# Where small VectorE operations stand in an attention loop: the first batch's routing and the early conversions moved to the steps that carry products of P and v

## The chip, the cores and the metric

The kernel runs on 1 core of one Trainium2 chip. The metric is the device time of one execution in microseconds. TensorE (PE) does the matrix products and transposes, VectorE (DVE) and ScalarE (ACT) the elementwise work, GpSimd (POOL) elementwise work and some DMAs, SyncE (SP) issues most DMAs. Each engine works through its own list of instructions in order and waits for others by semaphores.

## The reference

Three parts run one after the other (fp32 results):

```python
# attention over 2 batches, 8 heads, 768 tokens, 64 wide, masked by cluster
q_assign = argmax(normalised q . centroids); k_assign = the same for k
scores = where(q_assign == k_assign, q @ k.T / 8, -1e9)
x = softmax(scores) @ v              # -> 1536 tokens x 512
# mixture of 8 experts, each token to the one with the largest logit
e_idx = argmax(x @ w_gate)
x = gate * sigmoid(x @ w_output_gate)[e_idx] * (relu(x @ w1[e]) @ w2[e])
# dense block
h = x @ w_in;  out = (h * sigmoid(1.702 h)) @ w_out     # 512 -> 2048 -> 512
```

`w_in` and `w_out` arrive as float64.

## The kernel before

**The attention loop.** The work of two heads of a batch is a unit, eight units in all (0 to 3 batch 0, 4 to 7 batch 1). A unit has 12 steps, so the loop variable `i` runs over 96 steps and two more; a step is 128 queries of one head. Here a step's place in its unit is r, so that i = 12u + r. The order of instructions on every engine is written by hand (`manual_schedule`). In one pass of the loop at `i` these are issued: the scores of step i+1 on PE (L515, L516) and their row maximum on DVE (`nm`, L518); small pieces of preparation for the next unit; in some passes a few conversion operations (`convert_early`); one entry of `av`, a third of a unit's products of P and v (PE, L567), if one is queued; the transposes of step i-1 (PE, L532), each half copied out of PSUM by ACT (L537) and by DVE (L539), in `emit_pt`; and the exponential of step i+1 on ACT (L524). The scores have two PSUM buffers, so scores of a step wait for the exponential of two steps before. The transposes have two PSUM buffers of half a step each.

**Steps with products.** From unit 1 on, `av` holds something in the passes r = 2, 3, 8 and 9 (every third step and the one after it), 24 PE instructions each. In r = 3 and 9 the product's result is then copied by ACT (`oa`, L573). At r = 2 the cluster scores of the next unit follow (PE, `pcl`, L418), which DVE transposes (L421) and works on (L391 to L400). At r = 9 ACT makes the rows `ohT` (L429) and SP sends eight small DMAs (L435) into `Q` and `Z` of the next unit. At r = 10, 11, 0 and 1 the next unit's q and k are transposed on PE (`pqk`, L337), in the PSUM buffer of the products, which is free when `oa` has been copied.

**Routing of the first batch.** `route(0)` is a generator that chooses an expert for each of the first 768 tokens, ranks them and computes places. It is appended to `routing` at i = 61 and advanced by `advance(2)` after each of the two copies in `emit_pt`, so four parts a step. A part is mostly one DVE operation of a few columns. Three empty parts (`WAITS`) stand ahead of its small matmuls `prk`. Some of its operations (`sbase`, `srev8`, `span`, `soon`) give the address at which a block of fp32 rows is read later; SP reads `soon` in registers at i = 78. At the end six blocks of rows `xs` are scaled on POOL (L741) and scattered by POOL's indirect DMAs (L746), four parts each.

**Conversions.** The first two of the eight pieces of w_in and w_out are converted from float64 bits to fp32 during the attention. They are eight loads of 128x1024 words (`raw`), two of them held at a time. Each has four operations: `bits` (ACT squares the high words into `csq`, L125; DVE shifts, L126), `top` (L129), `tail` (L132), and `last`, which is DVE's `guard` on `csq` (L135), POOL's DMA of `csq` to DRAM (L176, `wd`) and the next load on SP (L113). `slots` says how many operations a pass issues. The target of the square is one buffer until i = 48, then two in turn:

```python
            hold, ops = wide_ops(cva, t, spare_squares[(4 * c + g) % len(spare_squares)])
...
        if i == NS // 2:
            assert len(fill) == E
            spare_squares.append(zrow)
```

After the attention come the second batch's routing, the experts and the dense block; nothing in them is edited.

Of the kernel before, what the change touches and what calls it, by code (L numbers as in the profile page):

```python
# [14 lines left out]
ALU = mybir.AluOpType  # L15
AX = mybir.AxisListType
# [7 lines left out]
E = 8  # L24
DFF = 2048
T = S // 128
# [20 lines left out]
def attention_moe_ffn(ctx: ExitStack, tc: tile.TileContext, q, k, v, centroids, w_gate, w_og, w1, w2, w_in, w_out, out):  # L47
    nc = tc.nc
# [11 lines left out]
    rev8 = const.tile([128, E], F32, name="rev8")  # L60
    ebase = const.tile([128, E], F32, name="ebase")
    iota8 = const.tile([128, E], F32, name="iota8")
# [16 lines left out]
    soon = const.tile([1, 2], I32, name="soon")  # L79
    gone = const.tile([128, E], F32, name="gone")  # L80
    ngone = const.tile([128, 1], F32, name="ngone")
    sbase = const.tile([128, E], F32, name="sbase")
    srev8 = const.tile([128, E], F32, name="srev8")
    span = const.tile([128, 3], F32, name="span")
    soonh = const.tile([128, E], F32, name="soonh")
# [79 lines left out]
    def convert_early():  # L165
        if not convert:
            if not ready:
                return
            c, g, t = ready.popleft()
            if not spare_squares:  # L170
                spare_squares.append(cva.tile([128, 512], F32, name="csq", tag="csq", bufs=1))
            hold, ops = wide_ops(cva, t, spare_squares[(4 * c + g) % len(spare_squares)])

            def last(f=ops[3]):
                f()
                nc.gpsimd.dma_start(out=wd[2 * c + g // 2][:, (g % 2) * 512:(g % 2) * 512 + 512], in_=hold["s"])  # L176
                load_early()
            convert.extend(ops[:3] + [last])
        convert.popleft()()
# [311 lines left out]

    TAIL, WAITS = 3, (3, 2, 0)
    BITS = (3, 10, 3)
    steps = [(u, h, j) for u in range(len(UNITS)) for h in range(2) for j in range(T)]

# [1 line left out]
    NS = len(steps)  # L499
# [26 lines left out]
    def emit_pt(i):  # L526
        L = live[i]
        j = steps[i][2]
        for n in range(2):
            pt = ps_t.tile([128, 512], F32, name="pt", tag="pt")  # L530
            for r in range(3):
                nc.tensor.transpose(pt[:, r * 128:(r + 1) * 128], L["P"][:, n, r * 128:(r + 1) * 128], ident)  # L532
            src = pt[:, :384].rearrange("p (r c) -> p r c", r=3)
            qs = slice(128 * (j % 3), 128 * (j % 3) + 128)
            dst = L["pT"][:, 3 * n:3 * n + 3, qs]
            if n == 0:
                nc.scalar.copy(dst, src)  # L537
            else:
                nc.vector.tensor_copy(dst, src)  # L539
            advance(2)  # L540

    KTS = (range(0, 3), range(3, T))
    av = deque()
# [52 lines left out]


    rt = {}


    GROUPS = ((0, 0, T), (1, 0, T // 2), (1, T // 2, T // 2))
# [4 lines left out]
    def route(gi):  # L606
# [62 lines left out]
        if gi == 0:  # L669
            nc.vector.tensor_tensor(dest, rk, ebase[:, None, :].to_broadcast([128, nj, E]), op=ALU.add)  # L670
            lm, lv, c0 = new("lm", [128, 1]), new("lv", [128, E]), new("c0", [128, E])
            nc.vector.tensor_copy(c0, part)
            yield
            nc.vector.scalar_tensor_tensor(lk, c0, float(E), rev8, op0=ALU.mult, op1=ALU.add)
            yield
            nc.vector.tensor_reduce(lm, lk, op=ALU.max, axis=AX.X)
            yield
            nc.vector.tensor_scalar(soonh, lk, lm, None, op0=ALU.is_equal)
            yield
            nc.vector.tensor_tensor(lv, soonh, c0, op=ALU.mult)  # L680
            yield
            nc.vector.tensor_reduce(ngone, lv, op=ALU.add, axis=AX.X)
            yield
            nc.vector.tensor_scalar(ngone, ngone, float(FIRST), None, op0=ALU.min)
            yield
            nc.vector.tensor_scalar(gone, soonh, ngone, None, op0=ALU.mult)
            yield
            nc.vector.scalar_tensor_tensor(sbase, gone, -1.0, ebase, op0=ALU.mult, op1=ALU.add)
            yield
            nc.vector.scalar_tensor_tensor(srev8, gone, -float(E), rev8, op0=ALU.mult, op1=ALU.add)  # L690
            yield
            nc.vector.tensor_tensor(lv, soonh, ebase, op=ALU.mult)
            yield
            nc.vector.tensor_reduce(span[:, 1:2], lv, op=ALU.add, axis=AX.X)
            yield
            nc.vector.tensor_tensor(span[:, 0:1], span[:, 1:2], ngone, op=ALU.subtract)
            yield
            nc.vector.tensor_copy(soon[:, 1:2], span[0:1, 0:1])
            nc.vector.tensor_tensor(lv, soonh, iota8, op=ALU.mult)
            yield  # L700
            nc.vector.tensor_reduce(lm, lv, op=ALU.add, axis=AX.X)
            yield
            nc.vector.tensor_copy(soon[:, 0:1], lm[0:1])
            yield
            nc.vector.tensor_tensor(dest, dest, gone[:, None, :].to_broadcast([128, nj, E]), op=ALU.subtract)
        else:
            nc.vector.tensor_tensor(dest, rk, sbase[:, None, :].to_broadcast([128, nj, E]), op=ALU.add)
# [16 lines left out]
        if gi == len(GROUPS) - 2:  # L724
            lm, lv = new("lm", [128, 1]), new("lv", [128, E])
# [6 lines left out]
        for j in range(nj):  # L732

            if b == 0:
                xs = pp.tile([128, DM], F32, name="xs", tag="xs", bufs=2)
            else:
                xs = xw[0][:, j0 + j].rearrange("p h c -> p (h c)")[:, :DM]
            dst = xs.rearrange("p (h d) -> p h d", h=H)
            src, g = xw[b][:, j0 + j, :, 0:D], gate[:, j:j + 1]
            if gi == 0:  # L740
                nc.gpsimd.tensor_scalar(dst, src, g, None, op0=ALU.mult)  # L741
            elif gi == 1 or j % 2:
                nc.scalar.activation(dst, src, AF.Copy, scale=g)
            else:
                nc.vector.tensor_scalar(dst, src, g, None, op0=ALU.mult)
            x = nc.gpsimd.indirect_dma_start(  # L746
                out=xd[:, :], out_offset=bass.IndirectOffsetOnAxis(ap=di[:, j:j + 1], axis=0),
                in_=xs, in_offset=None).ins
            nc.gpsimd.engine_nop()
            tc.declare_no_dep(x, group="rows", reason="every token has a row of its own")  # L750
            tc.add_to_no_dep_group("rows", x)
            for _ in range(3 if gi == 0 else 0):
                yield
            for y in fill:
                tc.add_manual_dep(x, y.name, DATA_DEP, reason="rows are zero first")
            scatters.append(x.name)
            yield

    sooner = {}

# [84 lines left out]
    def advance(n=1000, stop=0):  # L845
        while n > 0 and routing:
            n -= 1
            x = next(routing[0], 0)
            if x == 0:
                routing.pop(0)  # L850
            elif x == stop:
                break
# [77 lines left out]
            for f in pieces[u][n]:  # L930
                f()

    slots = {12 * u + r: n for u in range(2, 6) for r, n in ((3, 1), (8, 1), (9, 2))}
    slots.update({21: 3, 27: 1, 75: 1, 80: 1, 81: 2, 86: 3, 87: 2, 92: 2, 93: 2})

    weights = soon_weights()
    soon_at = {78: [soon_ids], 84: [soon_rows, lambda: next(weights)], 87: [lambda: next(weights)], 91: [soon_x]}
# [17 lines left out]
    for i in range(NS + 2):  # L955
        nu, r = divmod(i + 3, 12)
        if i == 3 or r == 0 and nu + 2 < len(UNITS):
            load_unit(nu + 2)
        prepare(i, True)
        if i + 1 < NS:  # L960
            emit_scores(i + 1)
        tail = i >= NS - TAIL
        if (tail or i % 3 == 0) and ost:
            ost.popleft()()
        prepare(i)
        if i == 0:
            spots[:] = [(ps_m, "m")]
        if i >= 14 and i % 4 == 2 and len(fill) < E:
            zero_rows(len(fill))
        if i % (NS // 2) == NS // 2 - 4 and i < NS:  # L970
            sum_logits(i // (NS // 2))
        if i == NS // 2 + 13:
            routing.append(route(0))
        for f in soon_at.get(i, ()):
            f()
# [3 lines that stand above are left out]
        if i in (15, 18):  # L979
            load_early()  # L980
        for _ in range(slots.get(i, 0)):
            convert_early()
        for _ in range(2 if tail else 1):
            if av:
                av.popleft()()
        prepare(i, False, True)
        if 0 <= i - 1 < NS:
            emit_pt(i - 1)
        n = i - (1 if tail else 2)
        if 0 <= n < NS and steps[n][2] % 3 == 2:  # L990
            queue_av(n)
        if i + 1 < NS:
            emit_exp(i + 1)
# [358 lines left out]
    with tc.manual_schedule():  # L1352
# [14 lines left out]
        for g in range(G + 2):  # L1367
            e, c = divmod(g, 8)
            nxt = wins.get(e + 1)
            r = c - (7 - nxt["nr"]) if nxt else 0  # L1370
# [94 lines left out]
    with tc.manual_schedule():  # L1465
        gq = deque()
        for g in range(len(seq) + 2):
# [6 lines left out]
            if g >= 2:  # L1474

                for m in range(4) if g < len(seq) or g == len(seq) + 1 else ():
                    cuts = (slice(0, DM // 2), slice(DM // 2, DM)) if g == len(seq) + 1 and m == 3 else (slice(0, DM),)
                    for cs in cuts:
                        for g0, gh, gl in list(gq)[:1] if g < len(seq) else gq:
                            fh, tb, c, i = seq[g0]  # L1480
# [47 lines left out]
```

## Time and profile before

| what | value |
|---|---|
| time, median of 3 runs | 724.02 us (720.78 to 724.78) |
| time of the profiled execution | 724.04 us |
| span of its trace | 722.3 us |
| PE / PEld / DVE / ACT / POOL busy | 97% / 80% / 63% / 54% / 37% of the span |
| units 4, 5 and 6 of the attention | 29.50, 31.53 and 31.02 us |

The span runs from the first to the last instruction; the profiled execution's own time is 1.74 us longer. Busy shares are means over parts with different limits: PE is busy nearly all of the attention, DVE more in the attention than later. Times of a unit run from the start of its first row maximum to the next unit's first.

### The profile page before, as it was taken

The page shows a single profiled execution, that of the slowest core. Times are in us where ns is not written, and L with a number is a line of the kernel's source. Part 1 is how long each engine was busy: PE and PEld are TensorE (multiplying, and loading weights), DVE is VectorE, ACT ScalarE, POOL GpSimd, SP SyncE. Part 2 cuts the span into 40 slices and gives each one's busy share as a digit, 9 for nine tenths or more (in the row PEclk, how much of TensorE's full clock was granted, in tenths as well). Part 3 has the DMA queues.
Part 4 walks back from the last instruction along what each step waited for, and adds up shares of the span by engine and source line. Part 5 has one row for each costly group of instructions (what it writes and reads, how often), then busy time and mean ns, then how long its engine had stood idle before and what let it go on. Part 6 is the DMA issues. An engine that isn't in the chain of part 4 may idle for free.

```text
span 722.3 us, 12542 instructions
## 1 busy us (share of the span) xinstructions
PE 699.4 (97%) x4522; PEld 577.7 (80%) x4522; DVE 452.2 (63%) x888; ACT 393.0 (54%) x789; POOL 266.4 (37%) x219
## 2 busy tenths in 40 slices
PE   8999999999999998999999998999999999999996
PEld 6777776776766777999999898888888888888885
DVE  6969788899988972344544545788564666242322
ACT  7767676666766643566777676544434353222220
POOL 2230321303280033766979889222532112020202
PEclk8999999999999998999999999999999999999999
DMA  6768869546066538566677775233634220010101
GB/s 198 170 189 273 215 225 282 153 146 181 27 171 213 196 126 269 172 229 206 199 241 232 263 235 188 89 110 68 85 59 59 60 87 30 1 59 1 59 0 59
DMA packets 70573, 105.18 MB, mean 146 GB/s; under 512 B 9627, under 2 KB 48283, under 8 KB 70507
## 3 DMA queue, kind: packets, MB, share of 16 engines
q1 hardware_dynamic: 67563, 95.94, 45.7%
q0 software_dynamic: 2944, 8.40, 3.1%
q8 instruction: 37, 0.61, 0.3%
q14 instruction: 29, 0.24, 0.1%
HBM read 70.46 MB, written 14.69 MB: 118 GB/s over the span
## 4 chain that ended last, share of the span: by engine, by line
PE 54%; issue 17%; POOL 7%; DMA 7%; DVE 6%; ACT 6%; SPq 1%; POOLq 0%; ACTq 0%; DVEq 0%
PE po L567 6%; PE pt L532 5%; PE ph L1347 4%; PE ph L1349 4%; PE ph L1348 4%; PE py L1447 3%; PE py L1445 3%; PE py L1446 3%; PE sp L515 3%; PE sp L516 3%; POOL w L1067 3%; PE py L1162 3%; PE ph L1162 2%; ACT w L1064 2%; DMA raw<-in_moe_w_dram 2%
## 5 line engine op out<-in xcount | busy, mean ns | idle before, releaser
L1067 POOL TENSOR_TENSOR w<-raw,w 128x1024 fp32r<-128x1024 f32 x51 | 128.1, 2529 | 38.3 <-ACT w L1064 25.4
L518 DVE TENSOR_REDUCE nm<-sp 128x1 f32<-128x768 f32 x96 | 91.6, 955 | 15.6 <-PE sp L516 14.4
L1430 DVE TENSOR_TENSOR sg<-ph,sg 128x512 f32<-128x512 f32 x48 | 33.2, 691 | 99.7 <-ACT sg L1429 97.5
L524 ACT ACTIVATE P<-sp,nm 128x768 f32<-128x768 f32 x96 | 87.2, 909 | 10.6 <-DVE nm L518 10.1
L532 PEld LDWEIGHTS pt<-ident,P 128*128 128x128 f32 x576 | 65.2, 141 | 27.3 <-issue 16.9
L532 PE MATMUL pt<-ident,P 128*128 128x128 f32 x576 | 82.9, 277 | 3.4 <-DVE pT L539 1.6
L1429 ACT ACTIVATE sg<-ph 128x512 f32<-128x512 f32 x48 | 28.7, 597 | 104.8 <-PE ph L1349 100.4
L1447 PE MATMUL py<-w,gl 128*128 128x512 f32 (+1 forms) x194 | 75.2, 387 | 0.0
L1445 PE MATMUL py<-w,gh 128*128 128x512 f32 (+1 forms) x194 | 75.0, 387 | 0.0
L1446 PE MATMUL py<-w,gh 128*128 128x512 f32 (+1 forms) x194 | 75.0, 387 | 0.0
L1100 POOL TENSOR_TENSOR w<-csq,w 128x512 fp32r<-128x512 f32 x24 | 32.7, 1363 | 114.5 <-ACT w L1099 114.5
L1347 PE MATMUL ph<-yth,w 128*128 128x512 f32 x192 | 74.8, 390 | 0.0
L1349 PE MATMUL ph<-yth,w 128*128 128x512 f32 x192 | 74.7, 389 | 0.0
L1348 PE MATMUL ph<-ytl,w 128*128 128x512 f32 x192 | 74.7, 389 | 0.0
L515 PE MATMUL sp<-X,Q 128*128 128x384 f32 x192 | 73.6, 384 | 0.5 <-ACT P L524 0.4
L1162 PE MATMUL py<-ht,w 128*128 128x512 f32 (+6 forms) x224 | 69.8, 367 | 3.5 <-DVE room L1169 2.0
L1064 ACT CAST w<-raw 128x1024 fp32r<-128x1024 f32 x68 | 70.5, 1042 | 4.8 <-issue 2.5
L1162 PE MATMUL ph<-t,w 128*128 128x512 f32 (+6 forms) x224 | 68.9, 366 | 1.2 <-DVE ht L1186 0.7
L567 PE MATMUL po<-pT,ld_v 128*32 128x384 f32 x768 | 68.6, 490 | 0.0
L516 PE MATMUL sp<-Z,Q 80*128 80x384 f32 x192 | 65.3, 340 | 1.9 <-DMA Q<-ohT 1.9
L537 ACT COPY pT<-pt 128x384 f32<-128x384 f32 x96 | 45.9, 478 | 32.7 <-PE pt L532 32.7
L539 DVE COPY pT<-pt 128x384 f32<-128x384 f32 x96 | 52.8, 550 | 8.1 <-PE pt L532 7.7
(294 smaller groups left out, 1468.7 us busy)
## 6 DMA issues: line engine op xcount, KB each, us to landing
raw<-in_moe_w_dram SPq DMA_DIRECT2D x64, 512.0 KB
raw<-in_moe_w_in_dram SPq DMA_DIRECT2D x16, 512.0 KB
raw<-in_moe_w_out_dram SPq DMA_DIRECT2D x16, 512.0 KB
xd<-zrow SPq DMA_DIRECT2D x8, 768.0 KB
Q<-Hq SPq DMA_DIRECT2D x28, 192.0 KB
ew<-in_moe_w_dram SPq DMA_DIRECT2D x9, 384.0 KB
ld_q<-in_q_dram SPq DMA_DIRECT2D x8, 384.0 KB
ld_k<-in_k_dram SPq DMA_DIRECT2D x8, 384.0 KB
```

The lines of the kernel that those rows point to most:

```text
L515: nc.tensor.matmul(sp[:, n, :384], d["Q1"][:, h, cs], d["X"][:, h, ks], start=True, stop=False)
L518: nc.vector.tensor_reduce(nm, sp[:, :, :384], op=ALU.max, axis=AX.XY, negate=True)
L532: nc.tensor.transpose(pt[:, r * 128:(r + 1) * 128], L["P"][:, n, r * 128:(r + 1) * 128], ident)
L567: nc.tensor.matmul(po[32 * g:32 * g + 32, :384], v_[:, hh, tile_t(kt), 32 * a:32 * a + 32], pts[n][:, kt, :], start=kt < (2 if alone else ...
L1067: (eng or nc.gpsimd).tensor_tensor(lo, r, f32(hi), op=ALU.subtract)
L1162: nc.tensor.matmul(ps[:, :2 * n], w_hi, t, start=first, stop=False)
L1347: nc.tensor.matmul(ph, wa(key, 0, k, i), yth[:, k, cs], start=(k == 0), stop=False)
L1348: nc.tensor.matmul(ph, wa(key, 0, k, i), ytl[:, k, cs], start=False, stop=False)
L1349: nc.tensor.matmul(ph, wa(key, 1, k, i), yth[:, k, cs], start=False, stop=(k == 3))
L1445: nc.tensor.matmul(po[m][:, cs], gh[:, ms], wb(key, 0, i)[:, cs], start=first, stop=False)
L1446: nc.tensor.matmul(po[m][:, cs], gh[:, ms], wb(key, 1, i)[:, cs], start=False, stop=False)
L1447: nc.tensor.matmul(po[m][:, cs], gl[:, ms], wb(key, 0, i)[:, cs], start=False, stop=last)
```

## The change

The routing of batch 0 starts at i = 56, no longer at 61, and is no longer advanced in `emit_pt` (only the passes of the last six steps still are). A table `PACE` says how many parts a pass issues, ahead of the products: 4 at i = 56, 5 at 57, 8 at 62, 5 at 68 and one at each of 69 to 76. The three empty parts and those between scatters are gone. The nine operations for the fp32 rows' address become `soon_place`, issued at i = 74. Conversions move: `slots` gains passes at r = 2 and loses those at r = 8 from unit 4 on. The 32 operations stand in these passes, as pass:count. Before: 21:3, 27:1, 32:1, 33:2, 39:1, 44:1, 45:2, 51:1, 56:1, 57:2, 63:1, 68:1, 69:2, 75:1, 80:1, 81:2, 86:3, 87:2, 92:2, 93:2. After: 21:3, 26:2, 27:1, 32:1, 33:2, 38:2, 39:1, 44:1, 45:2, 50:2, 51:1, 63:1, 69:2, 81:2, 86:3, 87:2, 92:2, 93:2.

```diff
-    TAIL, WAITS = 3, (3, 2, 0)
+    TAIL, WAITS = 3, (0, 2, 0)
...
             else:
                 nc.vector.tensor_copy(dst, src)
-            advance(2)
+            if i >= NS - T:
+                advance(2)
...
     rt = {}
+    later = []
...
             nc.vector.tensor_scalar(gone, soonh, ngone, None, op0=ALU.mult)
             yield
-            nc.vector.scalar_tensor_tensor(sbase, gone, -1.0, ebase, op0=ALU.mult, op1=ALU.add)
-            yield
...
-            nc.vector.tensor_reduce(lm, lv, op=ALU.add, axis=AX.X)
-            yield
-            nc.vector.tensor_copy(soon[:, 0:1], lm[0:1])
-            yield
+            later.append((lm, lv))
             nc.vector.tensor_tensor(dest, dest, gone[:, None, :].to_broadcast([128, nj, E]), op=ALU.subtract)
...
-            for _ in range(3 if gi == 0 else 0):
-                yield
             for y in fill:
                 tc.add_manual_dep(x, y.name, DATA_DEP, reason="rows are zero first")
             scatters.append(x.name)
             yield
+
+    def soon_place():
+
+        lm, lv = later.pop()
+        nc.vector.tensor_tensor(lv, soonh, ebase, op=ALU.mult)
+        nc.vector.tensor_reduce(span[:, 1:2], lv, op=ALU.add, axis=AX.X)
+        nc.vector.tensor_tensor(span[:, 0:1], span[:, 1:2], ngone, op=ALU.subtract)
+        nc.vector.tensor_copy(soon[:, 1:2], span[0:1, 0:1])
+        nc.vector.tensor_tensor(lv, soonh, iota8, op=ALU.mult)
+        nc.vector.tensor_reduce(lm, lv, op=ALU.add, axis=AX.X)
+        nc.vector.tensor_copy(soon[:, 0:1], lm[0:1])
+        nc.vector.scalar_tensor_tensor(sbase, gone, -1.0, ebase, op0=ALU.mult, op1=ALU.add)
+        nc.vector.scalar_tensor_tensor(srev8, gone, -float(E), rev8, op0=ALU.mult, op1=ALU.add)
...
-    slots = {12 * u + r: n for u in range(2, 6) for r, n in ((3, 1), (8, 1), (9, 2))}
-    slots.update({21: 3, 27: 1, 75: 1, 80: 1, 81: 2, 86: 3, 87: 2, 92: 2, 93: 2})
+    slots = {12 * u + r: n for u in range(2, 6) for r, n in ((2, 2 if u < 5 else 0), (3, 1), (8, u < 4), (9, 0 if u == 4 else 2))}
+    slots.update({21: 3, 27: 1, 81: 2, 86: 3, 87: 2, 92: 2, 93: 2})
+
+    PACE = {8: 4, 9: 5, 14: 8, 20: 5, **{n: 1 for n in range(21, 29)}}
...
-        if i == NS // 2 + 13:
+        if i == NS // 2 + 8:
             routing.append(route(0))
...
             convert_early()
+        advance(PACE.get(i - NS // 2, 0))
+        if i == NS // 2 + 26:
+            soon_place()
         for _ in range(2 if tail else 1):
             if av:
                 av.popleft()()
```

## Rows read from the trace of the kernel before

**Rows 1.** Busy time by engine in units 4, 5 and 6 (us, count), then clock, DMA share, GB/s.

```profile
133.64:163.14 29.50, 29.32 (x250) 21.71 (x249) 24.85 (x41) 20.02 (x45) 6.56 (x10) 1.00 0.55 154
163.14:194.67 31.53, 29.85 (x258) 21.95 (x256) 29.90 (x80) 20.28 (x47) 7.43 (x9) 1.00 0.41 108
194.67:225.69 31.02, 29.31 (x248) 21.45 (x246) 25.21 (x41) 20.14 (x45) 21.08 (x20) 1.00 0.59 161
```

**Rows 2.** Waits of PE in unit 5: total us, times, longest.

```profile
PE pt L532 <- DVE pT L539: 0.9, 2, 0.5
PE prk L661 <- DVE cntb L639: 0.5, 1, 0.5
```

**Rows 3.** DVE's instructions by line in unit 5: busy us, mean ns, idle before.

```profile
L618 DVE TENSOR_TENSOR lgp<-lgp,xw 128x96 f32<-128x96 f32 x2 | 1.6, 814 | 0.0
...
L135 DVE SCALAR_TENSOR_TENSOR zrow<-zrow,ct 128x512 f32<-128x512 f32 x1 | 0.7, 682 | 0.0
...
L126 DVE TENSOR_SCALAR ct<-raw 128x512 int32<-128x512 int32 x1 | 0.4, 386 | 0.0
...
L634 DVE TENSOR_REDUCE cnt<-roh 128x8 f32<-128x48 bf16 x1 | 0.2, 239 | 0.0
```

**Rows 4.** Wait of PE in unit 6, the longest one.

```profile
PE sp L516 <- DMA Q<-ohT: 1.2, 1, 1.2
```

**Rows 5.** Timeline of SP near the end of unit 6: start us, us.

```profile
214.95 1.76 SPq L113 DMA_DIRECT2D raw<-in_moe_w_out_dram  x1
```

**Rows 6.** Timeline around pass i = 26: start us, us, idle before and releaser.

```profile
80.16 1.01 POOL L344 TENSOR_TENSOR Lk<-Fk,Hk 128x384 fp32r<-128x384 f32 x1
...
80.44 0.96 DVE L518 TENSOR_REDUCE nm<-sp 128x1 f32<-128x768 f32 x1 [0.22 <-PE sp L516]
...
83.12 0.58 DVE L421 STREAM_TRANSPOSE sc<-pcl 128x384 f32<-128x384 f32 x1 [1.72 <-PE pcl L418]
83.57 0.48 ACT L537 COPY pT<-pt 128x384 f32<-128x384 f32 x1 [2.79 <-PE pt L532]
...
83.94 0.91 ACT L524 ACTIVATE P<-sp,nm 128x768 f32<-128x768 f32 x1
...
87.20 0.42 PE L515 MATMUL sp<-X,Q 128*128 128x384 f32 x1
```

**Rows 7.** Timelines of POOL and ACT: three instructions on `csq` and `zrow`.

```profile
117.72 0.58 POOL L176 DMA_DIRECT2D wd<-csq  x1 [7.01 <-DVE rs L577]
...
125.58 0.69 ACT L125 ACTIVATE csq<-raw 128x512 f32<-128x512 f32 x1 [0.24 <-DMA wd<-csq]
...
177.62 0.56 POOL L176 DMA_DIRECT2D wd<-zrow  x1 [7.86 <-DVE rs L576]
```

**Rows 8.** POOL's DMA queue from 178.8 to 179.8 us: packets, MB, share.

```profile
q0 software_dynamic: 72, 0.23, 60.8%
```

**Rows 9.** The chain of waits in unit 5, one piece: start us, us.

```profile
171.56 3.66 DMA X<-Hk
```

**Rows 10.** Two stretches, columns as in rows 1.

```profile
82.00:84.00 2.00, 2.00 (x24) 1.18 (x17) 0.84 (x2) 0.43 (x2) 0.00 (x0) 1.00 0.90 242
102.00:104.00 2.00, 2.00 (x17) 1.93 (x16) 1.65 (x3) 1.95 (x5) 0.64 (x2) 1.00 0.15 37
```

**Rows 11.** Timeline around pass i = 33: start us, us, idle before and releaser.

```profile
99.68 0.68 DVE L129 SCALAR_TENSOR_TENSOR ct<-raw,ct 128x512 int32<-128x512 int32 x1
...
100.83 0.48 ACT L573 COPY oa<-po 128x384 f32<-128x384 f32 x1 [1.17 <-PE po L567]
...
101.66 0.91 ACT L524 ACTIVATE P<-sp,nm 128x768 f32<-128x768 f32 x1
...
102.12 0.49 PE L337 MATMUL pqk<-ident,ld_q 128*128 128x128 f32 x3
...
103.03 0.42 PE L515 MATMUL sp<-X,Q 128*128 128x384 f32 x1
```

**Rows 12.** Timeline of DVE after pass i = 56.

```profile
157.08 0.56 DVE L539 COPY pT<-pt 128x384 f32<-128x384 f32 x1 [0.47 <-PE pt L532]
```

More of the change, by code (lines that the diff above doesn't have):

```diff
@@ L687, in route @@
             yield
-            nc.vector.scalar_tensor_tensor(sbase, gone, -1.0, ebase, op0=ALU.mult, op1=ALU.add)
-            yield
-            nc.vector.scalar_tensor_tensor(srev8, gone, -float(E), rev8, op0=ALU.mult, op1=ALU.add)
-            yield
-            nc.vector.tensor_tensor(lv, soonh, ebase, op=ALU.mult)
-            yield
-            nc.vector.tensor_reduce(span[:, 1:2], lv, op=ALU.add, axis=AX.X)
-            yield
[L696 to L700, printed above, removed]
-            nc.vector.tensor_reduce(lm, lv, op=ALU.add, axis=AX.X)
-            yield
-            nc.vector.tensor_copy(soon[:, 0:1], lm[0:1])
-            yield
+            later.append((lm, lv))
             nc.vector.tensor_tensor(dest, dest, gone[:, None, :].to_broadcast([128, nj, E]), op=ALU.subtract)
@@ L751, in route @@
             tc.add_to_no_dep_group("rows", x)
-            for _ in range(3 if gi == 0 else 0):
-                yield
             for y in fill:
```

## The prediction

> **What bounds the kernel now.** I read the page first: PE is busy nearly everywhere, so an edit in the attention counts only where PE stands still or is stretched. Then I compared units by stretch, because the 12 steps of a unit repeat and an undisturbed unit is a ready measure of what the others lose. In [rows 1] unit 4 takes 29.50 us with 29.32 us of PE, unit 5 31.53 with 29.85, unit 6 31.02 with 29.31. The reader should see that units 5 and 6 are 2.03 and 1.52 us longer at the same full clock, and that DVE is busy for 29.90 of unit 5's 31.53 us. Third came PE's waits: in unit 5 they name DVE, the copy `pT` (0.9 us) and the cast `cntb` (0.5 us) [rows 2]; in unit 6 one wait of 1.2 us for the small DMAs into `Q` [rows 4]. Last came the timelines of the passes that receive the moved work.
>
> **What the change takes away.** Unit 5 holds the routing of batch 0: two additions of 0.81 us and some 36 small operations of at most 0.24 us [rows 3], which I count at 0.15 to 0.2 us each, between the copies that PE waits for. After the change no routing stands between copies there. What PE still does for it, 7 small matmuls, is about the 0.5 us by which unit 5's PE time exceeds unit 4's [rows 1]. So unit 5 gains 2.03 - 0.5 = 1.5 us (at most 2.0, at least 0.9 if only the waits on `pT` go).
>
> Unit 6 loses the `guard` at i = 75 and `bits` at 80, and the early load that is issued at 214.95 behind unit 7's stacked rows [rows 5]. That load of 0.5 MB runs just ahead of the small DMAs that PE then waits for. After the change it is issued at i = 69, before those rows. I take the whole wait, 1.2 us [rows 4]; bounds 0 (other transfers, POOL's scatters too, are late as well) and the 1.5 us by which the unit is long.
>
> **What the moved DVE work costs.** At r = 2 DVE waits 1.72 us for `pcl` [rows 6]. That idle time covers `guard` and `bits` at i = 26 and 50 (0.68 + 0.39 = 1.07 us [rows 3]), `top` and `tail` at 38 (two like the 0.68 us of [rows 11]), ten routing parts at 62 (ten by some 0.18 = 1.8 us) and the nine of `soon_place` at 74 (nine by 0.15 = 1.4 us). I cost them at nothing; without the cover they would be delays of 1.1 to 1.8 us each on the next row maximum. At i = 56 the two additions and two small operations make 1.63 + 0.4 = 2.0 us, against 0.39 us of `bits` removed and 0.47 us that the copy waits for PE [rows 12]: DVE falls 1.2 us behind. At 57 seven parts of 0.2 us replace `top` and `tail`, no change; at 68 eight of 0.18 us give 0.6 us of lag; at 69 1.07 us replaces 1.4. The lag meets a maximum whose exponential is not needed at once, so I take 0.3 us in all, between 0 and 1.8.
>
> At no cost: the scatters stay one a step in 69 to 74, since four parts a step with three empty ones became one. POOL does the same 12 instructions; its `wd` at 69 comes ahead of the first scatter, where it stood behind the last. `soon` is ready at 74, four passes before SP reads it; SP's queue behind it (the row DMAs) is not needed until unit 7. The removed empty parts are no instructions.
>
> **What the moved conversions add: ACT waits for a DMA.** Until i = 48 there is one target for the square, and piece 4 takes it again. At i = 26, 33 and 50 the pass issues `last` of one piece and `bits` of the next, both on `csq`. ACT's square must not overwrite `csq` before POOL's DMA has read it. That this wait is real is in [rows 7]: the DMA issued at 117.72 held the square back until 125.58, 7.9 us later, and it was five passes before. In the changed passes the two are in one pass, so ACT stands for the whole of DVE's `guard`, POOL's issue and the transfer. Behind it on ACT stand the copy `pT` and the exponential, and at i = 33 also `oa`; PE waits for all three.
>
> Let L be the time from the issue of `wd` to ACT's release. The lower bound is 2.1 us: issued at 177.62 in a quiet stretch [rows 7], its packets were through by 179.8 [rows 8]. The upper is 7.9 us.
>
> At i = 26 the maximum ends at 81.40, `guard` at 82.0, POOL is free (its L344 ends at 81.17), so `wd` starts at 82.1 [rows 6]. The square takes about 0.65 us, the copy 0.37 until the exponential starts, the exponential 0.91: it ends at 82.1 + L + 1.93 = 84.0 + L. The scores that need its buffer ran at 87.20 [rows 6]. PE loses L - 3.2 us. The DMA engines are 0.90 busy there [rows 10], with transfers of 192 KB; one of these took 3.66 us after its issue [rows 9]. `wd` has 256 KB, a third more, so I take L = 4.5: 1.3 us lost. Pass 50 has the same pattern in unit 4: another 1.3 us. The bounds are 0 and 4.7 us each.
>
> At i = 33 `guard` would stand where `top` starts, 99.68, end at 100.36, and `wd` start at 100.45 [rows 11]. The DMA engines are only 0.15 busy [rows 10], so L is near its lower bound, 2.2 us. The square runs from 102.65 to 103.3, `oa` to 103.7, `pT` to 104.1, the exponential to 105.0. The transposes `pqk`, which reuse the products' buffer, ran at 102.12 and would wait for `oa` until 103.7; the scores at 103.03 would wait until 105.0 [rows 11]. The larger counts: 2.0 us. With L = 4 it is 3.8 us. ACT has `oa` and, in the following passes, copies of `pqk` to do as well and does not catch up before PE has lost the time.
>
> The Trainium skill, in "DMA: Bandwidth & Descriptors", section "Anatomy of one DMA — SWDGE (gpsimd) path", gives a GpSimd DMA about 2.0 us plus its bytes over 436e3 per us; for 256 KB an estimate of 2.6 us. The quiet transfer agrees with it roughly, the one of 7.9 us does not. By that page the passes 26 and 50 would cost nothing and the sum below would be about 2 us lower, which is the first rival.
>
> **The sum.** Lost: 1.3 + 1.3 + 2.0 + 0.3 = 4.9 us. Gained: 1.5 + 1.2 = 2.7 us. Net 2.2 us longer. Against the profiled execution, 722.3 us of span and 1.74 us around it, 724.04 in all: 726.2 us. The median of the three runs is 724.02, so the same forecast holds for it. The attention ends before the experts' loads and products start, so I carry its difference to the end one to one. Differences under 0.5%, 3.6 us, can hardly be told from none.
>
> **Rivals.**
> *The transfers are short.* If L is at most 3.2 us at passes 26 and 50, only pass 33 costs: 2.0 + 0.3 - 2.7 = -0.4, or 723.6 us. For it speaks the quiet transfer [rows 7, 8], against it the DMA share of 0.90 [rows 10]. Chance 0.17. This is the case of the page's estimate.
> *The transfers are long.* If `wd` queues behind the stacked rows and loads as the one at 117.72 did, L is 7 at 26 and 50 (3.8 us each) and 4 at 33 (3.8): 11.4 + 0.3 - 2.7 = 9.0, or 733.0 us, slower. It decides from a total of waits of 6.0 us on, which with pass 33 as computed is L above 5.2. For it: two of the three passes lie where the DMA engines are nearly full; against it: 3.66 us for a smaller transfer in such a stretch [rows 9]. Chance 0.15.
> *PE has enough other work.* If the products that stand in these very passes cover all three waits and no DVE lag appears, the change does what it looks like: 2.7 to 3.5 us gained, 720.9 us. The 2.79 us that ACT waits for PE at r = 2 [rows 6] speak for it; at r = 9 there is only 1.17 us [rows 11], against it. Chance 0.13.
> *The forecast*, 726.2 us, has 0.55. Its own range is 723.5 to 729.5 (L from 3.5 to 6, the wait in `Q` gone or not).
>
> **Numbers.** The range 721.2 to 731 leaves out half of the last rival and most of the long transfers' upper part, about 0.2. Faster by over 0.5% (under 720.4) needs that last rival with unit 6 gaining more than its wait: 0.1 with what I may have overlooked. Slower by over 0.5% (over 727.6): the long transfers, 0.15, and the upper third of the forecast, 0.18: 0.33. The rest, 0.57, is no change that can be told.
>
> **What would show it.** Right: waits of ACT's L125 on the DMA of `wd` at three places, each 2 us or more, and behind them PE waits on ACT's `P`, `pT` or `oa` near passes 26, 33 and 50; units 2, 3 and 4 longer than 29.5 us by 1 to 2.5 us, unit 5 near 30.0, unit 6 near 29.8, no wait of L516 on `Q` in it. Wrong: no wait on L125, or one without a PE wait behind it; DVE's idle time at r = 2 gone and `nm` late in units 4 and 6; units 5 and 6 as long as before.

## The result and the profile after

The changed kernel takes 728.93 us (median of 16 executions, 723.5 to 733.75), the kernel before 723.3 us (16 executions, 720.76 to 727.6). The ratio is 1.0074 with an interval of 1.0054 to 1.0094, so the change costs about 5.4 us. The forecast was a cost of 2.2 us; the 728.93 us lie in its range of 721.2 to 731. The profiled execution has a span of 729.0 us at a mean granted clock of 0.983, against 722.3 us at 0.989 before.

The windows of units 2 to 6 (columns as in [rows 1]):

```profile
74.49:108.70 34.21, 30.48 (x250) 22.04 (x248) 26.16 (x44) 20.10 (x45) 7.14 (x11) 0.98 0.74 217
108.70:139.41 30.71, 30.54 (x251) 22.94 (x250) 27.07 (x44) 20.12 (x45) 6.31 (x10) 0.96 0.79 234
139.41:170.87 31.46, 29.60 (x251) 21.75 (x249) 26.31 (x51) 19.84 (x46) 6.59 (x10) 1.00 0.52 145
170.87:200.65 29.78, 29.61 (x258) 22.00 (x256) 26.75 (x59) 20.33 (x46) 8.46 (x10) 1.00 0.38 96
200.65:230.04 29.39, 29.06 (x248) 21.43 (x245) 25.76 (x48) 18.95 (x43) 19.91 (x19) 1.00 0.57 160
```

Units 5 and 6 lose what made them long: 31.53 becomes 29.78, 31.02 becomes 29.39 [rows 1], together 3.38 us gained. Units 2, 3 and 4 pay: unit 4 goes from 29.50 [rows 1] to 31.46 us, unit 2 is at 34.21 us. Units 2 and 3 also show a clock below 1.00. The waits of PE in units 2 to 6 (total us, times, longest) say for whom it stands:

```profile
PE pt L532 <- ACT pT L537: 3.6, 2, 1.8
PE pqk L337 <- ACT oa L574: 1.9, 1, 1.9
PE pt L532 <- DVE pT L539: 0.7, 3, 0.3
PE sp L516 <- DMA Q<-ohT: 0.2, 1, 0.2
```

Three new waits on ACT's copies make 5.5 us. The wait for `Q` is down from 1.2 us [rows 4] to 0.2. The timelines of POOL, ACT, PE and DVE at passes 26, 33 and 50 show what ACT stood for (start us, us, in brackets the idle time before and its releaser):

```profile
82.26 0.78 POOL L176 DMA_DIRECT2D wd<-csq  x1 [1.15 <-DVE csq L135]
...
83.06 0.58 DVE L421 STREAM_TRANSPOSE sc<-pcl 128x384 f32<-128x384 f32 x1 [0.66 <-PE pcl L418]
...
87.19 0.69 ACT L125 ACTIVATE csq<-raw 128x512 f32<-128x512 f32 x1 [6.47 <-DVE m L400]
87.79 0.46 ACT L537 COPY pT<-pt 128x384 f32<-128x384 f32 x1
88.15 0.89 ACT L524 ACTIVATE P<-sp,nm 128x768 f32<-128x768 f32 x1
...
88.30 0.87 PE L532 MATMUL pt<-ident,P 128*128 128x128 f32 x6 [1.73 <-ACT pT L537]
89.18 0.44 PE L515 MATMUL sp<-X,Q 128*128 128x384 f32 x1
...
102.42 0.57 POOL L176 DMA_DIRECT2D wd<-csq  x1 [19.38 <-DVE csq L135]
...
104.86 0.66 ACT L125 ACTIVATE csq<-raw 128x512 f32<-128x512 f32 x1 [3.45 <-DVE pT L539]
105.42 0.47 ACT L574 COPY oa<-po 128x384 f32<-128x384 f32 x1
...
105.94 0.55 PE L337 MATMUL pqk<-ident,ld_q 128*128 128x128 f32 x3 [1.92 <-ACT oa L574]
...
147.17 0.56 POOL L176 DMA_DIRECT2D wd<-csq  x1 [1.13 <-DMA Q<-Hq]
...
152.23 0.68 ACT L125 ACTIVATE csq<-raw 128x512 f32<-128x512 f32 x1 [6.59 <-DVE nm L518]
...
153.32 0.87 PE L532 MATMUL pt<-ident,P 128*128 128x128 f32 x6 [1.82 <-ACT pT L537]
```

The reader is to see one chain three times: POOL issues `wd`, ACT stands idle until the square may overwrite `csq`, and behind the square come the copy and PE. L, the time from the issue to the square, is 87.19 - 82.26 = 4.93 us at pass 26, 2.44 at pass 33 and 5.06 at pass 50. The brackets of the squares name DVE instructions. DVE's `m` (L400) ended at 86.35 us in unit 2, but it gives ACT nothing that the square needs: a wait for several things is put to the one that came last by the records. That the DMA holds the square is shown by run e8 below, where the bracket names it, and by e1, where another buffer takes the wait away. The Trainium skill, in "DMA: Bandwidth & Descriptors", section "Anatomy of one DMA — SWDGE (gpsimd) path", would give an estimate of 2.6 us for such a transfer. Pass 33 agrees with it, the two passes in loaded stretches do not.

The DVE row shows the cover at r = 2: it waits 0.66 us for `pcl`, where it waited 1.72 [rows 6]. The missing 1.06 us are the `guard` and `bits` that now stand there, and cost nothing.

What was not foreseen stands right behind pass 33. Three windows, before, in and after 3.4 us of it (the third column from the end is the granted clock):

```profile
105.00:107.00 2.00, 1.05 (x9) 0.96 (x9) 0.09 (x1) 2.00 (x5) 0.00 (x0) 1.00 0.15 37
107.60:111.00 3.40, 3.40 (x16) 3.30 (x15) 1.55 (x3) 2.79 (x6) 2.60 (x4) 0.50 0.94 276
111.00:113.00 2.00, 2.00 (x17) 2.00 (x16) 1.52 (x3) 0.56 (x3) 0.41 (x1) 1.00 0.96 311
```

PE idles for 1.92 us until 105.94, and from 107.6 to 111.0 us its granted clock is 0.50, that is 1.2 GHz instead of 2.4, while it is busy without a gap. The same work takes some 1.7 us longer. Before, no unit from 2 to 6 has such a stretch.

### The profile page after: what moved, and what is told of

It is laid out like the page before. It is cut to its first block, busy times and chain, and to the rows that moved or that the text cites. A ratio compares the mean times of both kernels' runs of the same rounds, so it can differ in the third digit from the quotient of the medians.

```text
span 729.0 us, 12545 instructions
## 1 busy us (share of the span) xinstructions
PE 703.1 (96%) x4522; PEld 580.3 (80%) x4522; DVE 454.3 (62%) x888; ACT 392.8 (54%) x789; POOL 266.1 (37%) x219
## 4 chain that ended last, share of the span: by engine, by line
PE 65%; issue 16%; DVE 6%; POOL 4%; ACT 4%; DMA 4%; POOLq 0%; SPq 0%; ACTq 0%; DVEq 0%
PE pt L532 8%; PE po L568 7%; PE sp L515 5%; PE sp L516 4%; PE ph L1349 4%; PE ph L1351 4%; PE ph L1350 4%; PE ph L1164 4%; PE py L1164 3%; PE py L1449 3%; PE py L1448 3%; PE py L1447 3%; POOL w L1069 3%; DMA raw<-in_moe_w_dram 2%; PE pox L587 2%
```

## The experiments

The runs are numbered e1 to e8. Five of them (e1, e2, e3, e5, e8) name the target of each piece's square in a tuple; the change itself has one target until i = 48 and two in turn from there. The buffer `csqb` lies where another one (`cblk`) is no longer needed, so it costs no memory.

**e1: two targets in turn.** All of the change, but at passes 26, 33 and 50 the square has another buffer than the DMA.

```diff
+                spare_squares.append(one.tile([128, 512], F32, name="csqb", tag="cblk"))
+                spare_squares.append(zrow)
-            hold, ops = wide_ops(cva, t, spare_squares[(4 * c + g) % len(spare_squares)])
+            hold, ops = wide_ops(cva, t, spare_squares[(0, 1, 0, 1, 0, 2, 0, 2)[4 * c + g]])
...
-            spare_squares.append(zrow)
```

> The change with a second target for the square: pieces 1 and 3 square into a buffer of their own, so that no pass has a DMA from and a square into the same buffer. Theory (ACT's waits on the DMA of csq cost the time): no wait of L125, units 2 to 4 back at 29.5 us each, units 5 and 6 as short as in the change (29.8 and 29.4), so 2.5 to 3.5 us under the kernel before, ratio 0.995 to 0.997. Rival (the moved DVE operations or the earlier loads cost it, the waits are covered by products): as slow as the change, ratio 1.006 to 1.008.

Measured: 721.59 us, ratio 0.9978 [0.9961, 0.9995]. The windows of units 2, 4, 5 and 6:

```profile
73.21:102.84 29.63, 29.45 (x251) 21.73 (x249) 25.89 (x43) 20.74 (x46) 7.39 (x11) 1.00 0.80 243
...
132.80:162.32 29.52, 29.35 (x251) 21.75 (x249) 26.09 (x52) 19.83 (x44) 6.16 (x10) 1.00 0.56 154
162.32:192.09 29.77, 29.60 (x257) 21.99 (x256) 26.73 (x59) 20.32 (x46) 8.45 (x10) 1.00 0.38 97
192.09:221.45 29.36, 29.04 (x248) 21.41 (x245) 25.76 (x48) 18.94 (x43) 19.89 (x19) 1.00 0.58 160
```

The buffer alone turns a loss of 0.7% into a gain of 0.2%. Units 2 to 6 take 29.4 to 30.0 us (unit 3 the longest, 29.96), no PE wait on ACT and no low clock is left in them, while units 5 and 6 keep their gains. In unit 4 the moved routing and conversions together cost nothing.

**e2 and e3: each wait by itself.** The tuple is (0, 0, 1, 0, 0, 2, 0, 2) in e2, where the waits at passes 26 and 50 stay, and (0, 1, 1, 0, 1, 2, 0, 2) in e3, where only the one at pass 33 does.

> The change with the second target used by piece 2 alone: the waits at passes 26 and 50 stay, that at 33 goes. Theory: the two waits cost 1.8 us each, the half clock near 108 us is gone with the wait at 33, and with 3.4 us gained in units 5 and 6 the time is within 1 us of the kernel before, 4 us under the change. Rival (the clock falls because of the sum of stalls, not that one): the half clock stays and only 2 us go.

> The change with the second target used by pieces 1, 2 and 4: only the wait at pass 33 stays. Theory: it costs 4 us, 2 of them by the wait and 2 by the half clock behind it, so unit 2 is 32 to 33.5 us, the half clock stays, and the time is 0.5 to 1.5 us over the kernel before. Rival (the clock fell only because pass 26 had stalled too): no half clock, 2 us lost, 1.4 us under the kernel before.

Measured: e2 725.13 us, 1.0022 [1.0004, 1.0039]; e3 724.85 us, 1.0018 [1.0001, 1.0036]. PE's waits in units 2 to 4 and the windows of units 2 and 4 of e2, then the wait and the window of unit 2 of e3:

```profile
PE pt L534 <- ACT pT L539: 2.7, 2, 1.6
...
73.69:104.58 30.89, 29.71 (x251) 21.75 (x249) 26.13 (x43) 20.46 (x46) 7.50 (x11) 1.00 0.77 233
...
134.19:165.42 31.23, 29.63 (x251) 21.76 (x249) 26.33 (x51) 19.80 (x46) 6.52 (x10) 1.00 0.53 146
```

```profile
PE pqk L339 <- ACT oa L576: 1.9, 1, 1.9
...
74.51:106.50 31.99, 29.82 (x251) 21.68 (x249) 25.94 (x44) 20.01 (x44) 6.49 (x10) 1.00 0.76 229
```

Against e1, pass 26 costs 30.89 - 29.63 = 1.26 us here, pass 50 costs 31.23 - 29.52 = 1.71, and pass 33 costs 31.99 - 29.63 = 2.36, all at full clock. By the ratios, e2 is 0.0044 and e3 0.0040 above e1; added to e1 they make 1.0062, near the change's 1.0074: within the intervals the costs add up. Two expectations failed in part. e2 is 1.6 us over the kernel before, where at most 1 was expected, and the half clock expected in e3 is absent from its profiled execution, though its time is as expected.

**e4 and e5: one half of the change each.** e4 is the change with the `slots` of before, so only the routing moves. e5 is the kernel before with the `slots` of the change and the two targets of e1, so only the conversions move, without a wait.

```diff
 e4 (against the change)
-    slots = {12 * u + r: n for u in range(2, 6) for r, n in ((2, 2 if u < 5 else 0), (3, 1), (8, u < 4), (9, 0 if u == 4 else 2))}
-    slots.update({21: 3, 27: 1, 81: 2, 86: 3, 87: 2, 92: 2, 93: 2})
+    slots = {12 * u + r: n for u in range(2, 6) for r, n in ((3, 1), (8, 1), (9, 2))}
+    slots.update({21: 3, 27: 1, 75: 1, 80: 1, 81: 2, 86: 3, 87: 2, 92: 2, 93: 2})
```

> The routing of the first batch as in the change, the conversions in the passes of the kernel before. Theory: no pass has both uses of csq, no wait at 26, 33, 50; unit 5 is 1.0 to 1.7 us shorter than before, unit 6 keeps its wait for the small DMAs of 1.2 us: 1 to 2 us under the kernel before. Rival (the gain of units 5 and 6 comes from the conversions that left them, not from the routing): unit 5 as long as before, 31.5 us, and no difference in time.

> The conversions in the passes of the change with a second target, the routing of the kernel before (from i = 61, in the copies). Theory: no wait on csq; unit 6 loses its wait for the small DMAs, 29.4 us; unit 5 keeps the routing between the copies and stays over 30.5 us, less some of the 0.7 us that the conversions in passes 56, 57 and 68 cost: 1 to 2 us under the kernel before. Rival (unit 6's gain comes from the routing's move): unit 6 stays at 31 us.

Measured: e4 721.34 us, 0.9971 [0.9952, 0.9991]; e5 721.8 us, 0.9998 [0.9974, 1.0022]. In e4 units 4, 5 and 6 take 30.64, 29.70 and 30.67 us; in e5 29.53, 31.96 and 29.41. So unit 5's gain is the routing's, and unit 6's comes with the conversions alone (e5). In time, e5 shows none of the 1 to 2 us that were expected. With the conversions left at i = 56 and 57, the routing that starts there costs unit 4 1.1 us; in e1, where both are moved, it costs nothing. The change needs both halves. Unit 6 of e4 stays long for another reason than the expected one. Its PE waits hold no `Q`, but the first line here; the second is an operation on DVE just ahead of the copy:

```profile
PE pt L532 <- DVE pT L539: 1.6, 1, 1.6
...
206.62 0.96 DVE L577 TENSOR_SCALAR rs<-sm 128x6 f32<-128x6 f32 x1
```

DVE's copy at pass 75 is late behind `guard` (0.68 us) and this operation, which took 0.96 us here and 0.16 in the median. `soon_place` is not the reason: it ended at 200.9 us, and DVE then stood idle for 0.94 us. Why the operation took so long is open, so e4 doesn't tell what unit 6 would take without it.

**e6: the change again**, beside the runs of the next two, to see what repeats.

> The change itself once more. If the half clock near 108 us belongs to it, it is there again, behind the wait of pass 33, and pass 33 costs 4 us again; if it comes in some executions only, the wait of 1.9 us at pass 33 stays and the half clock can be gone, with a span 1.7 us shorter. The ratio to the kernel before is 1.005 to 1.009 in either case.

Measured: 726.2 us, 1.0051 [1.0025, 1.0077]. PE's waits in units 2 to 6, and the windows of two stretches:

```profile
PE pt L532 <- ACT pT L537: 2.9, 2, 1.8
PE pqk L337 <- ACT oa L574: 1.9, 1, 1.9
...
105.10:108.50 3.40, 3.40 (x15) 3.30 (x16) 0.63 (x2) 2.73 (x7) 1.50 (x2) 0.50 0.51 133
152.90:156.30 3.40, 3.38 (x14) 3.27 (x13) 1.92 (x3) 2.67 (x6) 0.00 (x0) 0.50 0.87 283
```

The same three waits, but here half clock follows those at passes 33 and 50; after pass 26 (1.06 us) there is none.

**e7: PE kept busy during the wait of pass 33.** The change, with nine products of zeros whose result nobody reads.

```diff
+        if i == 34:
+            z = ps_m.tile([128, 512], F32, name="fill", tag="m")
+            for _ in range(9):
+                nc.tensor.matmul(z, idle[:, 0:128], idle, start=True, stop=True)
         prepare(i)
```

> The change with 9 products of zeros (128x512, bf16) on PE ahead of the transposes of pass 34, that is in the wait of 1.9 us behind pass 33; their result goes to a PSUM tile that nothing reads. If PE's idling there brings the half clock, there is none, and the time is 1 to 2 us under the change. If the half clock has nothing to do with it, or is not in most executions, the time is that of the change within 0.5 us.

Measured: 728.72 us (6 executions), 1.0087 [1.0055, 1.0119]; not faster than the change, so the expected gain of 1 to 2 us failed to come. At pass 33 there is neither a PE wait nor a low clock. But in this execution it follows the waits at passes 26 and 50:

```profile
90.40:93.80 3.40, 3.40 (x14) 3.30 (x15) 1.93 (x3) 2.81 (x7) 0.00 (x0) 0.51 0.93 292
155.30:158.70 3.40, 3.40 (x15) 3.21 (x14) 1.68 (x3) 2.60 (x6) 0.00 (x0) 0.50 0.96 308
```

**e8: one such wait at a new place.** Targets (0, 1, 0, 1, 0, 0, 2, 0): passes 26, 33 and 50 are free, and the pass at i = 69, in unit 5, has the DMA and the square on one buffer.

> The change with the second target, but pieces 4 and 5 on one target, so that a wait on the DMA of csq stands at pass 69 alone, in a stretch where the DMA engines are quiet (r = 9, as pass 33). Theory: the wait of L125 is 3 to 3.5 us, the transfer some 2.2 to 2.5 of it, PE waits about 1.9 us for oa or more, unit 5 or 6 grows by 2 to 2.5 us: ratio 1.000 to 1.002. Rival (the loss of pass 33 belonged to its surroundings, not to the target): no loss, ratio 0.997 as with two targets.

Measured: 724.16 us, 1.0024 [0.9999, 1.0049]. Timelines of POOL and ACT, and the windows of unit 5 and of the stretch behind the wait:

```profile
189.67 0.56 POOL L178 DMA_DIRECT2D wd<-csq  x1 [19.66 <-DVE csq L135]
...
192.06 0.66 ACT L125 ACTIVATE csq<-raw 128x512 f32<-128x512 f32 x1 [3.38 <-DMA wd<-csq]
192.62 0.46 ACT L576 COPY oa<-po 128x384 f32<-128x384 f32 x1
...
163.40:196.69 33.29, 31.27 (x257) 23.38 (x256) 26.80 (x59) 20.49 (x47) 10.33 (x13) 0.95 0.42 111
193.00:196.40 3.40, 3.26 (x13) 3.17 (x14) 0.56 (x1) 3.09 (x8) 1.76 (x4) 0.50 0.69 207
```

Here the releaser is named: the DMA of `csq`, L = 2.39 us. Unit 5 takes 33.29 us instead of e1's 29.77: 3.5 us for one wait, half clock included. By the ratios e8 is 0.0046 above e1, 3.3 us.

**The clock over all executions.** One execution's trace shows one outcome, but each execution has its mean granted clock. A span of some 725 us with PE busy all through would lose about 725 x (1 - clock); one stretch of 3.4 us at half clock lowers the mean by 3.4 x 0.5 / 725 = 0.0023 and costs 1.7 us. Over the 12 executions of e6, time and clock have a correlation of -0.94, from 722.7 us at 0.991 to 731.73 at 0.979; in the 16 of the change it is -0.85. Means over the executions:

| kernel | executions | mean us | mean clock | less before, us | of it clock, us | rest, us |
|---|---|---|---|---|---|---|
| before (with e1 to e4) | 35 | 723.69 | 0.9884 | | | |
| e1, no waits | 12 | 721.88 | 0.9887 | -1.8 | -0.2 | -1.6 |
| e2, passes 26 and 50 | 12 | 725.35 | 0.9883 | +1.7 | +0.1 | +1.6 |
| e3, pass 33 | 12 | 725.02 | 0.9870 | +1.3 | +1.0 | +0.3 |
| e4, routing alone | 12 | 721.62 | 0.9910 | -2.1 | -1.9 | -0.2 |
| before (with e5 to e8) | 29 | 722.03 | 0.9892 | | | |
| e5, conversions alone | 12 | 722.11 | 0.9892 | +0.1 | 0.0 | +0.1 |
| e6, the change | 12 | 726.16 | 0.9871 | +4.1 | +1.5 | +2.6 |
| e7, pass 33 filled | 6 | 729.00 | 0.9835 | +7.0 | +4.1 | +2.8 |
| e8, one wait at 69 | 12 | 723.96 | 0.9870 | +1.9 | +1.6 | +0.3 |

The clock column is 725 times the difference of the two mean clocks, the last column what is left. It counts too much: every profiled execution ends at half clock behind PE's last product, where it costs PE nothing, and this end makes 1.0 us of the loss before, 1.8 in the change and 2.2 in e6. So the clock column is a rough figure, here rather too high, and it doesn't say where in an execution the clock was low. By it e7's rest is that of the change, and nearly all of the excess is clock; e4's gain is mostly clock, and whether its routing makes the kernel faster is not shown.

## Why the prediction was right in kind and short in size

**Right: what the change adds.** ACT waits for the DMA of `csq` at the three passes named, PE waits behind it on `pT` and `oa`, and units 5 and 6 come out at 29.78 and 29.39 us where 30.0 and 29.8 were named. e1 shows that this reuse of one buffer is all that makes the change slow. The rival of enough other work on PE fell: no wait was covered. One sign was named wrongly: units 2, 3 and 4 were each to be longer. Passes 26 and 33 both lie in unit 2, which is 34.21 - 29.53 = 4.7 us longer than before; unit 3 (29.56 before) is longer by 1.15 us only because the half clock runs into it.

**Right in number: the formula at passes 26 and 50, with L a little short.** PE was to lose L - 3.2 us. With the measured L of 4.93 and 5.06 it gives 1.73 and 1.86; the waits are 1.73 and 1.82. The estimate L = 4.5 gave 1.3 each. The formula was worked out for another wait, though: for the scores, which need the exponential. PE stood one step earlier, at the transposes `pt`, for the copy `pT`. The two paths end almost together (the exponential ends at 89.04 us and the scores start at 89.18), which is why the formula still fits; that was luck. The rivals of a short transfer (3.2 at most) and a long one (7) both fell. Pass 33 was put at 2.0 and cost 2.36 in e3; there too PE stood at the earlier place, `pqk` for `oa` (1.92 us, where the working had 1.6).

**The sum.** Waits 1.73 + 2.36 + 1.82 = 5.9 us; gains 31.53 - 29.78 = 1.75 in unit 5 (1.5 was taken) and 31.02 - 29.39 = 1.63 in unit 6 (1.2 was taken); DVE's lag of 0.3 us was not seen (e1's unit 4 has 29.52 us). Part of unit 6's gain is given back in unit 7: from its first row maximum (225.69 us before, 230.04 in the change) to its last it takes 26.30 us before and 26.66 in the change.

```profile
251.99 0.96 DVE L518 TENSOR_REDUCE nm<-sp 128x1 f32<-128x768 f32 x1 [0.15 <-PE sp L516]
...
256.70 0.96 DVE L518 TENSOR_REDUCE nm<-sp 128x1 f32<-128x768 f32 x1 [0.15 <-PE sp L516]
```

That is 5.91 - 3.38 + 0.36 = 2.9 us, against 2.2 forecast: longer waits and larger gains partly cancel. The rest of e6 after the clock, 2.6 us, agrees with it as far as that column goes. Two figures of the working don't follow from its own terms: with passes 26 and 50 at no cost the sum is 2.6 us lower, as in the first rival, not about 2; and an L from 3.5 to 6 gives 724.2 to 729.2 us, or 730.4 with the wait in `Q` left, not 723.5 to 729.5.

**The step that failed: a lost microsecond of PE was counted once.** The sum had no term for the clock. In the profiled executions the waits on ACT at which PE stood idle for over 1 us are 12 (three each in the change and e6, two in e2 and e7, one in e3 and e8), and 6 of them were followed by 3.4 us at half clock; in units 2 to 6 of before, e1, e4 and e5 there is no such stretch. In the profiled execution of the change this is the 1.7 us behind pass 33. Another 1.7 us go in a second stretch, in the experts, which the change does not edit. There PE waits 1.4 us for DVE (`room`) in all ten profiled kernels. Half clock follows in the change, e2, e3, e6 and e8, and does not in before, e1, e4, e5 and e7. The wait before and in the change, and the stretch in the change:

```profile
441.30 0.39 PE L1162 MATMUL py<-ht,w 128*128 128x256 f32 x1 [1.42 <-DVE room L1169]
...
446.96 0.39 PE L1164 MATMUL py<-ht,w 128*128 128x256 f32 x1 [1.40 <-DVE room L1171]
...
448.90:452.30 3.40, 3.40 (x19) 3.40 (x18) 0.65 (x3) 2.96 (x6) 3.40 (x3) 0.50 0.99 360
```

So of the 6.7 us by which the profiled span is longer, 3.4 are half clock that the sum had at nothing, and only half of that stands behind a wait that the change made. Whether the change has to do with the other half is not shown. Over the executions the clock term is 1.5 us in e6. For the change's 16 executions the mean clock is 0.9846; against the 0.9884 of the kernel before in e1's runs it makes 2.8 us, and 5.4 - 2.8 = 2.6 us is left once more. Since that clock of before is from other executions, the 2.8 us is the weaker number of the two, and both hold some of the end at half clock that costs nothing.

**Not shown either way: that a gain is carried to the end one to one.** Units 5 and 6 of e1 gain 3.4 us, but its time, less the clock, only 1.6. Most of the difference lies in the attention: units 2, 3 and 7 of e1 are 0.10, 0.40 and 0.36 us longer than before, so 2.5 us are gained at its end. (In e1's profile the attention ends 3.9 us earlier, but 1.3 of these were there when unit 2 began, ahead of the moved work.) At the start of the experts PE's three waits ahead of the transposes `pxt` make 3.20 us in e1 and 2.06 before, so 1.1 us more are lost; but at the wait for `room` e1 is 3.6 us ahead again (437.73 against 441.30), and its span is 3.4 us shorter. That leaves 2.1 us of the 2.5, which the interval of e1's time, about 1.2 us either way, can't tell from 1.6. In e5 unit 6 is 1.6 us shorter and units 5 and 7 are 0.4 longer each; the 0.7 us left with the small changes of units 2 to 4 are within the interval of its time, 1.7 us either way. What holds the experts' first rows stays open.

**Open: which wait drops the clock.** The waits on ACT of 1.06 us (e6 at pass 26) and of 1.15 and 1.58 (e2) had no drop, but the wait of 1.4 us for `room` had it in five executions of ten. Those of 1.7 to 1.9 us had it in some executions and not in others: the one at pass 26 in e7 (1.69) but not in the change (1.73), the one at pass 33 in the change and e6 but not in e3 (1.9 in all). So the length of the wait alone does not decide, and that the waiting is what brings the drop is argued from the order in time. e7 doesn't settle it: its filled wait had no drop, but neither had the same wait unfilled in e3.

## What to carry to other kernels

Before moving the last use of a buffer and its next first use into one step, look at what reads the buffer: if it is a DMA, the engine that writes next stands for the whole transfer, in order, with everything queued behind it; one more buffer is the remedy, and e1 (0.9978) is the better form of this change. Where PE is busy nearly all the time, price a wait of PE at its length and then at what the clock may take: here one wait of 1.8 to 1.9 us cost about 3.5 us when the half clock followed. And add up a gain over all parts, not over those that the change is meant for: of e1's 3.4 us in units 5 and 6, 0.9 were lost again in units 2, 3 and 7.

## What the runs showed of the hardware

An idle time of PE of 1.7 to 1.9 us, between stretches in which it was busy nearly without a gap, was followed in 6 of 9 cases by 3.4 us at a granted clock of 0.50 or 0.51, beginning at PE's restart (e8: PE starts again at 193.14 us) up to 1.7 us behind it (the change: 107.6 against 105.94). One of 1.4 us in the experts was followed by such a stretch in five of ten profiled executions.

The same transfer of 256 KB by POOL held its buffer for 2.39 (e8) to 5.06 us. The windows of its three flights in the changed kernel (second column from the end: DMA share):

```profile
102.40:104.90 2.50, 1.63 (x14) 1.27 (x10) 1.76 (x5) 0.04 (x1) 0.57 (x1) 1.00 0.45 144
82.30:87.20 4.90, 4.27 (x46) 1.93 (x34) 4.13 (x9) 0.01 (x1) 0.74 (x1) 1.00 0.97 256
147.20:152.20 5.00, 4.30 (x46) 1.96 (x38) 4.24 (x9) 0.00 (x0) 0.53 (x1) 1.00 0.91 254
```

With the engines 0.45 busy, this transfer included, it took half of what it took at 0.91 to 0.97. ACT was idle in all three.
